# One small expert in plain fp32 and a shorter largest expert, in the second layer of an attention and two-MoE kernel

## The chip, the cores and the metric

One core of a Trainium2 chip runs the whole kernel. The metric is the device time of one execution in microseconds. Three runs of the kernel before gave 630.59, 633.81 and 631.4 us, a median of 631.4. The profile comes from one further execution.

## The reference, cut to what matters

Attention over chunks of 32 tokens is followed by two mixture-of-experts layers on 1536 tokens of 512 numbers, with 8 experts of 512 x 1024 and 1024 x 512 weights each. The first layer gives each token to two experts. The second one, which the change touches, gives each token to one:

```python
def _moe2_ref(x, w_gate, w1, w2, capacity):
    logits = x @ w_gate
    expert_idx = np.argmax(logits, axis=1)
    ...
    gate_w = probs[np.arange(N), expert_idx]
    ...
    h = np.maximum(np.einsum('ecd,edf->ecf', disp, w1), 0.0)
    y = np.einsum('ecf,efd->ecd', h, w2)
    ...
            out[i] = gate_w[i] * y[expert_idx[i], pos[i]]
```

The capacity is 384 tokens an expert. With the reference's inputs the second layer's experts get 215, 120, 35, 306, 113, 213, 369 and 165 tokens.

## The kernel before, in words

**Experts as jobs.** Each expert is a `Job` with a fixed number of slots, gathered by token number from DRAM into tiles `xg` of 128 rows. In the second layer one expert (369 tokens here) is done first, in two jobs. The other seven are ranked by their counts on the chip, and rank `s` gets `CAPS2[1 + s]` slots. They run in the order `ORDER2 = [0, 5, 1, 6, 2, 3, 4]`: the largest first, and the smallest (rank 6) fourth. Tokens that fit no slot would be done in blocks of 128 by `rest2` at the end, in a loop whose count is read from the data.

**Two kinds of job.** A product of fp32 numbers is made of three products of split ones: each operand is split into a high part `hi` in fp32r and a rest `lo`, and `mm3` (L804) adds lo x hi, hi x lo and hi x hi. A job of kind "M" (over 128 slots) does its first product by column blocks of the hidden layer, 8 units that stream the tokens (`layer1`, L815), and its second by blocks of 128 tokens, two units each, that stream 512 weight columns (`rows2`, L860). A job of kind "T" (up to 128 slots) has four units: `hidden` (L841) twice, with the tokens as stationary operand, 512 weight columns moving and a transposition `turn` (L849) of the result in the middle of the next unit, and `rows2` twice. After a unit, ScalarE takes the result out of PSUM (`hh`, `hr`, `hl` by VectorE), and `psA` has two buffers.

**Weights.** An expert's weights are four pieces of 1 MB. Piece n is loaded in two halves (`half`, L710) into four buffers `raww`, and split in four chunks (`split`, L738): ScalarE writes `whi`, VectorE `wlo`. Split pieces lie in five slots, "AAABC"[n % 5]. Which chunk is split after which unit of which job is a plan of numbers (`due`, L1667 to L1690); each second chunk then starts the load of the half four further on (`raw_next`). All weight loads are issued on SP's queue, gathers and scatters on POOL's.

**Order of the last jobs on TensorE's clock (us):** the largest ranked expert (384 slots) from 481.26, a 128-slot expert from 515.26, a 256-slot expert from 528.11, the smallest (128 slots) from 551.38, a 256-slot expert from 564.74, another from 588.54, and a 128-slot one from 611.50 to the end.

Of the kernel before, what the change touches and what calls it, by code (L numbers as in the profile page):

```python
# [8 lines left out]
F32 = mybir.dt.float32  # L9
# [3 lines left out]
I32 = mybir.dt.int32  # L13
# [2 lines left out]
AX = mybir.AxisListType  # L16

CAPS1 = [128, 432, 412, 404, 396, 384, 384, 384, 312]
CAPS2 = [256, 384, 256, 256, 256, 128, 128, 128, 128]
ORDER2 = [0, 5, 1, 6, 2, 3, 4]  # L20
NEG = -1.0e30
WARM = 7
# [32 lines left out]
def attention_two_moe_kernel(  # L55
# [698 lines left out]
    def x_block(xg, blk, C, tag="B", later=False):  # L754
        n = min(128, C - 128 * blk)
        p = bank(tag)
        pv = p.rearrange("p (k n) -> p k n", k=KD)
        for c in range(KD):
            nc.tensor.transpose(pv[:, c, 0:128], xg[:, c * 128:(c + 1) * 128], ident)  # L759
        o = slice(128 * blk, 128 * blk + n)  # L760
        xh, xl = st["x"]
        nc.scalar.activation(xh[:, :, o], pv[:, :, 0:n], AF.Copy)  # L762
        low = lambda: nc.vector.tensor_tensor(xl[:, :, o], pv[:, :, 0:n], xh[:, :, o], op=OP.subtract)  # L763
        if not later:
            low()
        return low
# [74 lines left out]
    def hidden(w, c, n, between=None):  # L841

        ps = bank("A")
        xh, xl = st["x"]
        mm3(ps[:n], [((xh[:, k, 0:n], xl[:, k, 0:n]), (w[0][:, k], w[1][:, k])) for k in range(KD)],
            between=between, order=RO)
        nc.scalar.activation(st["hr"][:n, 512 * c:512 * c + 512], ps[:n], AF.Relu)

    def turn(c, n):  # L849
# [7 lines left out]
        nc.scalar.activation(hh[:, o, 0:n], pv[:, :, 0:n], AF.Copy)  # L857
        nc.vector.tensor_tensor(hl[:, o, 0:n], pv[:, :, 0:n], hh[:, o, 0:n], op=OP.subtract)

    def rows2(n0, blk, half_, C, between=None):  # L860

        n = min(128, C - 128 * blk)
        s_ = slice(128 * blk, 128 * blk + n)
        if half_ == 0:
            st["l2"] = bank("C")
        hh, hl = st["h"]
        w = P[n0 + 2 + half_]
        mm3(st["l2"][:n], [((hh[:, 4 * half_ + f, s_], hl[:, 4 * half_ + f, s_]), (w[0][:, f], w[1][:, f]))
                           for f in range(4)], half_ == 0, half_ == 1, between, RO)
# [21 lines left out]
    def scatter(yr, n, ids_ap, first, prev):  # L891
        off = bass.IndirectOffsetOnAxis(ap=ids_ap[:n], axis=0)
        nc.gpsimd.memset(spacer, 0.0)
        if first:
            wr = nc.gpsimd.indirect_dma_start(out=x2_d, out_offset=off, in_=yr[:n], in_offset=None,  # L895
                                              compute_op=OP.add)
        else:
# [44 lines left out]
    class Job:  # L942


        def __init__(self, kind, n0, C, first, ids=None, gate=None, cols=None):
            self.kind, self.n0, self.C, self.first = kind, n0, C, first
            self.nb = -(-C // 128)
            self.ids, self.gate, self.cols, self.oids = ids, gate, cols, None
            self.W = W1 if first else W2
            self.late = None  # L950
            self.turns = {"W": [8, 10, 12, 14], "M": [8, 9, 10, 11], "T": TT}[kind]
            self.xg = None
            self.later = []
            self.pops = 4 if kind == "T" else 1
            self.quiet = 0 if kind == "T" else 1
            self.pool = ()
            self.weigh = 1 if kind == "T" else 5
            self.prev = []
            self.g = []
# [7 lines left out]
                self.xg.append(x)  # L967

        def x_block(self, blk, tag="B", gate=True):
            x_block(self.xg[blk], blk, self.C, tag)  # L970
            if gate:
                self.weight(blk)

# [26 lines left out]
        def units(self):  # L1000
            n0, C = self.n0, self.C
            if self.kind == "T":
                def between(c):
                    turn(c, C)
                    self.mid(c + 0.5)
                return [lambda: hidden(P[n0], 0, C), lambda: hidden(P[n0 + 1], 1, C, lambda: between(0)),
                        lambda: self.rows(0, 0, lambda: between(1)), lambda: self.rows(0, 1)]
# [288 lines left out]
    blkb = iota([128, NB1], [[128, NB1]], 0, 0, "blkb")  # L1296
    trash = iota([128, NB1 // 4, 4], [[0, NB1 // 4], [128, 4]], 0, 1, "trash")
    trash = trash.rearrange("p a b -> p (a b)")
    spacer = consts.tile([1, 1], F32, name="spacer")
    blank(1, nc.gpsimd)  # L1300
    v_blank(1)
# [58 lines left out]
    st["h"] = (wp["B"].tile([128, FB, CM], F32R, name="hh"), wp["B"].tile([128, FB, CM], F32R, name="hl"))  # L1360
    st["hr"] = wp["B"].tile([128, FF], F32, name="hr")
    st["yt"] = wp["B"].tile([128, KD, 128], F32, name="yt")
    st["y"] = (wp["B"].tile([128, KD, CM], F32R, name="yh"), wp["B"].tile([128, KD, CM], F32R, name="yl"))

    n2 = 4 * E
# [2 lines left out]
    kind2 = lambda c: "T" if c <= 128 else "M"  # L1368
    U0 = Job("M", n2, caps2[0], False, gate=lambda xg, g: gate2(xg, None, g))
    UL = Job("T", n2, caps2[E], False, gate=U0.gate)  # L1370
    R = [Job(kind2(caps2[1 + s]), n2 + 4 + 4 * i, caps2[1 + s], False, gate=U0.gate) for i, s in enumerate(ORDER2)]
    jobs = [V0, V8, *S, U0, UL, *R]
    at = {job: j for j, job in enumerate(jobs)}
# [218 lines left out]
    def chain2():  # L1592
        lt = late()
        w = ""
        while w != "counted":
            w = next(lt)
            if w != "counted":
                yield w
        yield "d"
        yield from turns(h_rank2(), lt)  # L1600
        kept = rt.tile([128, U0.nb], I32, name="kept")
        nc.vector.tensor_tensor(kept, tab2[:, E, 0:U0.nb], trash[:, 0:U0.nb], op=OP.add)
        ids, raw_ids = yield from slot_ids(tab2[:, 0:E], st["sel2"], E, NB2, "2")
        for job, s in zip(R, ORDER2):
            job.ids = [ids[:, s, b:b + 1] for b in range(job.nb)]
        for h in range(2 * n2 + 10, 2 * n2 + 12):
            raw(h, True)
        oids_u = out_ids(kept, tab2[:, E, 0:U0.nb], [128, U0.nb], rt, "u")
        U0.oids = [oids_u[:, b:b + 1] for b in range(U0.nb)]
        for f in U0.later:  # L1610
            f()
        yield "d"
        oids = out_ids(ids, raw_ids, [128, E, NB2], rt, "2")
        for job, s in [(UL, E - 1)] + list(zip(R, ORDER2)):
            job.oids = [oids[:, s, b:b + 1] for b in range(job.nb)]
        R[0].fetch()
# [51 lines left out]
        plan.setdefault((at[job], u), []).extend(what)  # L1668

    split_q += [(3, c) for c in range(4)]  # L1670
    for job in jobs[1:-1]:
        n = job.n0
        four = lambda m: [(m, c) for c in range(4)]
        if job is V8:
            todo_, us = four(4) + four(5) + four(6), [7, 7, 8, 8, 9, 9, 10, 11, 12, 13, 14, 15]
        elif job is U0:
            todo_, us = four(n + 3), [0, 1, 2, 3]
        elif job is UL:
            todo_, us = four(n + 4) + four(n + 5) + four(n + 6), UU
        elif job.kind == "T":  # L1680
            todo_, us = four(n + 4) + four(n + 5) + four(n + 6), US
        elif job.kind == "M":
            todo_ = sum((four(n + 3 + i) for i in range(4)), [])
# [5 lines left out]
        if job in R and jobs[at[job] + 1].kind == "T":  # L1689
            due(job, 6 + 2 * job.nb, *four(n + 7))  # L1690
    def raw_next(h):
        if h >= 8 and not 2 * n2 + 4 <= h < 2 * n2 + 8:
            raw(h + 4)

    run_jobs(jobs, hooks, lambda j, u: plan.get((j, u), []), raw_next)
    rest2(w1b, w2b, ov[2], en2, NB2)
# [36 lines left out]
```

## Time and profile before

| | |
|---|---|
| median of three runs | 631.4 us (630.59 to 633.81) |
| the profiled execution | 632.0 us |
| its span | 630.2 us |
| TensorE (PE) busy | 595.4 us, 94% of the span |
| VectorE (DVE) busy | 384.1 us, 61% |
| ScalarE (ACT) busy | 311.2 us, 49% |
| GpSimd (POOL) busy | 165.0 us, 26% |
| mean granted TensorE clock | 0.972 of 2.4 GHz |
| moved by DMA | 112.13 MB, mean 178 GB/s |

The span runs from the first to the last instruction of the profiled execution; its own time is 1.8 us longer. Busy times are sums over instructions with overlaps counted once. The page shows PE busy in nearly every slice of the second half, so what matters there is how long each stage of TensorE's work takes and where it waits.

### The profile page before, as it was taken

To read this page: it belongs to the slowest core of one execution; us is meant where nothing else is said; L and a number is where in the kernel's file an instruction comes from. 1 tells how busy PE (TensorE), PEld (TensorE's weight loads), DVE (VectorE), ACT (ScalarE), POOL (GpSimd) and SP (SyncE) were. 2 spreads that over 40 slices of the span, in tenths; PEclk is the share of its full clock that TensorE was granted. 3 is DMA by queue.
4 is the path that set the end of the run, shared out by engine and by line. 5 is a ranking of instruction groups with operands and counts; after the bars stand their busy time and mean duration, and the time that the engine had idled before them with its cause. 6 is when DMAs were issued, how large, how long until landed. Compare 5 with 4: busy or idle time off the path is not lost. (4 is left out here: it accounts for less than half of the span.)

```text
span 630.2 us, 12317 instructions
## 1 busy us (share of the span) xinstructions
PE 595.4 (94%) x4523; PEld 540.9 (86%) x4529; DVE 384.1 (61%) x1015; ACT 311.2 (49%) x653; POOL 165.0 (26%) x237
## 2 busy tenths in 40 slices
PE   7699869699999999999999999999999999999996
PEld 4688657499999999999999898988979988889984
DVE  8577754677645555555555447273557648687672
ACT  5265543225544544545445435344427557686563
POOL 8894000211411312313212130302351121111201
PEclk9799886899999999999999999999999999999999
DMA  9986670339775664856536565455366486776751
GB/s 252 269 142 197 214 234 20 88 99 345 222 221 168 174 185 149 221 152 135 170 103 151 166 142 165 107 121 151 38 235 215 152 264 220 251 273 234 247 182 41
DMA packets 77068, 112.13 MB, mean 178 GB/s; under 512 B 28353, under 2 KB 28353, under 8 KB 77000
## 3 DMA queue, kind: packets, MB, share of 16 engines
q1 hardware_dynamic: 68088, 88.99, 44.7%
q0 software_dynamic: 8912, 22.28, 15.7%
q8 instruction: 38, 0.62, 0.4%
q14 instruction: 30, 0.25, 0.1%
HBM read 88.90 MB, written 22.34 MB: 176 GB/s over the span
## 5 line engine op out<-in xcount | busy, mean ns | idle before, releaser
L746 DVE TENSOR_TENSOR wlo<-raww,whi 128x512 fp32r<-128x512 f32 x254 | 168.8, 688 | 44.1 <-ACT whi L745 42.7
L745 ACT ACTIVATE whi<-raww 128x512 fp32r<-128x512 f32 x256 | 152.2, 624 | 17.7 <-DMA raww<-in_moe_w_dram 14.9
L823 DVE SCALAR_TENSOR_TENSOR hl<-psA,hh 128x384 fp32r<-128x384 f32 (+6 forms) x104 | 54.0, 519 | 80.4 <-ACT hh L822 80.0
L822 ACT ACTIVATE hh<-psA 128x384 fp32r<-128x384 f32 (+6 forms) x104 | 47.7, 458 | 109.2 <-PE psA L811 109.2
L811 PE MATMUL psA<-xh,wlo 128*128 128x256 f32 (+6 forms) x416 | 85.8, 328 | 0.8 <-ACT xh L762 0.4
L811 PE MATMUL psA<-xh,whi 128*128 128x256 f32 (+6 forms) x416 | 83.7, 322 | 0.0
L811 PE MATMUL psA<-xl,whi 128*128 128x256 f32 (+6 forms) x416 | 83.6, 323 | 0.0
L895 POOL DMA_INDIRECT x_rows<-yr,ids x25 | 39.2, 1568 | 125.4 <-ACT whi L745 86.2
L811 PEld LDWEIGHTS psA<-xh,wlo 128*128 128x128 f32 x416 | 67.7, 190 | 2.4 <-ACT xh L762 0.8
L811 PEld LDWEIGHTS psA<-xl,whi 128*128 128x128 f32 x416 | 69.3, 189 | 0.6 <-DVEq L1098 0.2
L811 PEld LDWEIGHTS psA<-xh,whi 128*128 128x128 f32 x416 | 69.1, 189 | 0.4
L751 POOL DMA_INDIRECT xg<-x_rows,ids x37 | 37.1, 1002 | 100.7 <-DVE gs L931 41.1
L811 PE MATMUL psC<-wlo,hh 128*128 128x512 f32 x200 | 57.6, 407 | 0.0
L811 PE MATMUL psC<-whi,hh 128*128 128x512 f32 x200 | 55.6, 396 | 0.0
L811 PE MATMUL psC<-whi,hl 128*128 128x512 f32 x200 | 55.0, 395 | 0.0
L763 DVE TENSOR_TENSOR xl<-psB,xh 128x512 fp32r<-128x512 f32 (+4 forms) x37 | 23.9, 645 | 43.1 <-ACT xh L762 43.1
L811 PEld LDWEIGHTS psC<-whi,hh 128*128 128x128 f32 x200 | 37.4, 189 | 8.4
L811 PEld LDWEIGHTS psC<-whi,hl 128*128 128x128 f32 x200 | 37.5, 188 | 8.3
L762 ACT ACTIVATE xh<-psB 128x512 fp32r<-128x512 f32 (+4 forms) x37 | 20.7, 560 | 44.0 <-PE psB L759 41.8
L811 PEld LDWEIGHTS psC<-wlo,hh 128*128 128x128 f32 x200 | 35.4, 189 | 5.7
L898 POOL DMA_INDIRECT out_dram<-yr,oids x13 | 13.2, 1013 | 98.1 <-ACT yr L873 71.6
L811 PE MATMUL psA<-hh,wlo 128*128 128x312 f32 (+4 forms) x160 | 36.6, 350 | 0.0
(328 smaller groups left out, 913.3 us busy)
## 6 DMA issues: line engine op xcount, KB each, us to landing
raww<-in_moe_w_dram SPq DMA_DIRECT2D x128, 512.0 KB
x_rows<-zero SPq DMA_DIRECT2D x8, 520.0 KB
raw<-in_k_dram SPq DMA_DIRECT2D x6, 512.0 KB
raw<-in_q_dram SPq DMA_DIRECT2D x6, 512.0 KB
x_rows<-xs SPq DMA_DIRECT2D x12, 256.0 KB
out_dram<-zero SPq DMA_DIRECT2D x3, 1024.0 KB
v<-in_v_dram SPq DMA_DIRECT2D x10, 256.0 KB
x_rows<-zero SPq DMA_DIRECT2D x1, 1042.0 KB
```

What stands on the lines that cost most here:

```text
L745: nc.scalar.activation(hi[:, c], raw, AF.Copy)
L746: (eng or nc.vector).tensor_tensor(lo[:, c], raw, hi[:, c], op=OP.subtract)
L751: return nc.gpsimd.indirect_dma_start(out=xg, out_offset=None, in_=src, in_offset=bass.IndirectOffsetOnAxis(ap=ids_ap, axis=0))
L762: nc.scalar.activation(xh[:, :, o], pv[:, :, 0:n], AF.Copy)
L763: low = lambda: nc.vector.tensor_tensor(xl[:, :, o], pv[:, :, 0:n], xh[:, :, o], op=OP.subtract)
L811: nc.tensor.matmul(ps, w[a], x[b], start=first and i == 0, stop=last and i == n - 1)
L822: nc.scalar.activation(hh[:, f, 0:C], ps[:, 0:C], AF.Relu)
L823: nc.vector.scalar_tensor_tensor(hl[:, f, 0:C], ps[:, 0:C], 0.0, hh[:, f, 0:C], op0=OP.max, op1=OP.subtract)
L895: wr = nc.gpsimd.indirect_dma_start(out=x2_d, out_offset=off, in_=yr[:n], in_offset=None, compute_op=OP.add)
L898: wr = nc.gpsimd.indirect_dma_start(out=out, out_offset=off, in_=yr[:n, 0:DM], in_offset=None, bounds_check=N - 1, oob_is_err=False)
```

## The change

1. `CAPS2`: rank 0 gets 320 slots for 384, rank 6 gets 64 for 128.
2. The job with 64 slots is computed in plain fp32. `whole` loads each weight matrix as two tiles of 1 MB, unsplit, straight into the slots of pieces n and n+1; `halves` runs, for each of the row blocks, two matmuls with the same 64 tokens as stationary operand, one for the left 256 columns into partitions 0 to 63 of PSUM, one for the right 256 into 64 to 127. `hidden64`, `turn64` and `rows64` take the places of `hidden`, `turn` and `rows2`.
3. The tokens of that job are gathered twice (rows 0 to 63 and 64 to 127), and its output is scattered as half rows of 256 numbers with indices `2 * id + upper`.
4. The plan of splits is made to fit: pieces 50 and 51 are gone, the whole loads start during the 256-slot job ahead of the small one, and the 256-slot job behind it splits five pieces, not four.

```diff
-CAPS2 = [256, 384, 256, 256, 256, 128, 128, 128, 128]
+CAPS2 = [256, 320, 256, 256, 256, 128, 128, 64, 128]
+    def whole(n, two):
+        run_until(lambda: "C" in wp)
+        at_, ns = "AAABC"[n % 5], ("whi", "wlo")
+        P[n] = tuple(wp[at_].tile([128, 4, 512], F32, name=m, bufs=3 if at_ == "A" else 1) for m in ns)
...
+            nc.sync.dma_start(P[n][j], src)
+    def halves(ps, xs_, w, first, last, between):
+        for i, x in enumerate(xs_):
+            if between is not None and i == len(xs_) // 2:
+                between()
+            for d in range(2):
+                nc.tensor.matmul(ps[64 * d:64 * d + 64, 0:256], x, w[:, i, 256 * d:256 * d + 256],
+                                 start=first and i == 0, stop=last and i == len(xs_) - 1)
+            tick(0.4)
+    def hidden64(n0, c, between=None):
+        ps = bank("A")
+        halves(ps, [st["xf"][:, k] for k in range(KD)], P[n0][c], True, True, between)
+        nc.scalar.activation(st["hr"][:, 256 * c:256 * c + 256], ps[:, 0:256], AF.Relu)
+    def turn64(c):
+        p = bank("B")
+        for j in range(2):
+            nc.tensor.transpose(p[:, 128 * j:128 * j + 128], st["hr"][:, 256 * c + 128 * j:256 * c + 128 * j + 128],
+                                ident)
+        nc.scalar.activation(st["hf"][:, 4 * c:4 * c + 4].rearrange("p (d j) n -> p d j n", d=2),
+                             p[:, 0:256].rearrange("p (j d n) -> p d j n", j=2, d=2), AF.Copy)
+    def rows64(n0, c, between=None):
+        if c == 0:
+            st["l2"] = bank("C")
+        halves(st["l2"], [st["hf"][:, 4 * c + f] for f in range(4)], P[n0 + 1][c], c == 0, c == 1, between)
...
+        for t in (ids, raw_ids):
+            nc.vector.tensor_copy(t[64:128, HALF[0], 0:1], t[0:64, HALF[0], 0:1])
...
+        two = rt.tile([128, 1], I32, name="oids_h")
+        nc.vector.scalar_tensor_tensor(two, oids[:, HALF[0], 0:1], 2.0, upper, op0=OP.mult, op1=OP.add)
...
+    upper = iota([128, 1], [[0, 1]], 0, 1, "upper")
+    nc.gpsimd.tensor_scalar(upper, upper, 64.0, None, op0=OP.is_ge)
...
+    hook(R[HALF[1] - 1], 1, lambda: whole(nh, (HALF[0], 0)))
+    hook(R[HALF[1] - 1], 5, lambda: whole(nh + 1, (HALF[0], 1)))
...
+        elif job is hj:
+            todo_, us = four(n + 5), [1, 1.5, 2, 3]
...
+        elif jobs[at[job] + 1] is hj:
+            todo_, us = four(n + 3) + four(n + 8), [1, 2, 3, 4, 8, 9, 9, 10]
+        elif job.n0 == nh + 4:
+            todo_ = sum((four(n + 2 + i) for i in range(5)), [])
+            us = [0, 0, 1, 1, 2, 2, 3, 4, 5, 6, 7, 8, 8, 8, 9, 9, 10, 10, 11, 11]
...
-            raw(h + 4)
+            raw(h + 12 if 2 * nh - 4 <= h < 2 * nh else h + 4)
```

TensorE's order from the first matmul of the small expert to its second turning, in the kernel before (L811 is `mm3`, L855 `turn`, L759 the turning of the next expert's rows):

```order
L811 MATMUL psA<-wlo,xh 128x512 x4
L811 MATMUL psA<-whi,xh 128x512 x4
L811 MATMUL psA<-whi,xl 128x512 x4
L811 MATMUL psA<-wlo,xh 128x512 x4
L811 MATMUL psA<-whi,xh 128x512 x2
L855 MATMUL psB<-ident,hr 128x128 x4
L811 MATMUL psA<-whi,xh 128x512 x2
L811 MATMUL psA<-whi,xl 128x512 x4
L759 MATMUL psD<-ident,xg 128x128 x4
L811 MATMUL psC<-wlo,hh 128x512 x4
L811 MATMUL psC<-whi,hh 128x512 x2
L855 MATMUL psB<-ident,hr 128x128 x4
```

The small expert in the changed kernel, with the first matmuls of the next one at the end (L880 is `halves`, L894 `turn64`; whi and wlo hold the left and the right half of a weight matrix here):

```order
L880 MATMUL psA<-whi,xf 64x256 x8
L880 MATMUL psA<-wlo,xf 64x256 x4
L894 MATMUL psB<-ident,hr 128x128 x2
L880 MATMUL psA<-wlo,xf 64x256 x4
L759 MATMUL psD<-ident,xg 128x128 x4
L880 MATMUL psC<-whi,yt 64x256 x4
L894 MATMUL psB<-ident,hr 128x128 x2
L759 MATMUL psD<-ident,xg 128x128 x4
L880 MATMUL psC<-whi,yt 64x256 x4
L880 MATMUL psC<-wlo,yt 64x256 x8
L811 MATMUL psA<-xh,wlo 128x256 x4
```

48 matmuls of 512 columns and 16 transposes became 32 matmuls of 256 columns and 12 transposes; the transposes cut the new ones into four stretches.

ScalarE's order at the beginning of the 256-slot expert behind the small one, before (L745 is `split`, L822 the result of a `layer1` unit, L873 the small expert's rows):

```order
L873 ACTIVATE yr<-psC,gs 128x512
L745 ACTIVATE whi<-raww 128x512 x2
L822 ACTIVATE hh<-psA 128x256 x2
L745 ACTIVATE whi<-raww 128x512
L822 ACTIVATE hh<-psA 128x256
L745 ACTIVATE whi<-raww 128x512
L822 ACTIVATE hh<-psA 128x256
L745 ACTIVATE whi<-raww 128x512
L822 ACTIVATE hh<-psA 128x256
```

And in the changed kernel (L1069 is the small expert's rows):

```order
L1069 ACTIVATE yr<-psC,gs 128x256
L745 ACTIVATE whi<-raww 128x512
L822 ACTIVATE hh<-psA 128x256
L745 ACTIVATE whi<-raww 128x512 x2
L822 ACTIVATE hh<-psA 128x256
L745 ACTIVATE whi<-raww 128x512 x2
L822 ACTIVATE hh<-psA 128x256
L745 ACTIVATE whi<-raww 128x512 x2
L822 ACTIVATE hh<-psA 128x256
L745 ACTIVATE whi<-raww 128x512
L822 ACTIVATE hh<-psA 128x256
```

Each of the first three units is now followed by two conversions instead of one; VectorE's part `wlo` and its `hl` follow in the same order.

## Rows read from the trace of the kernel before

**Rows 1.** The page, busy us of an engine, its share and instructions.

```profile
PE 595.4 (94%) x4523; PEld 540.9 (86%) x4529; DVE 384.1 (61%) x1015; ACT 311.2 (49%) x653; POOL 165.0 (26%) x237
```

**Rows 2.** Windows over the second layer: stretch, length, busy us (instructions), clock, DMA.

```profile
core 0: us, PE busy (x) PEld busy (x) DVE busy (x) ACT busy (x) POOL busy (x), PEclk, DMA share, GB/s
481.00:498.00 17.00, 17.00 (x98) 16.93 (x97) 10.51 (x22) 8.70 (x20) 3.09 (x3) 1.00 0.65 218
...
528.00:551.00 23.00, 22.89 (x149) 20.64 (x148) 16.07 (x33) 14.27 (x32) 5.22 (x7) 1.00 0.78 261
```

**Rows 3.** Waits of PE from 400 to 632 us: total, times, longest.

```profile
PE psB L759 <- DMA xg<-x_rows,ids_ul: 0.9, 1, 0.9
...
PE psB L855 <- ACT hr L847: 0.3, 1, 0.3
```

**Rows 4.** Timeline of PE, largest expert: start, length, instructions, idle before.

```profile
481.26 0.86 PE L811 MATMUL psA<-xh,wlo 128*128 128x384 f32 x4
...
498.06 1.09 PE L811 MATMUL psC<-wlo,hh 128*128 128x512 f32 x4
```

**Rows 5.** Timeline of PE, first product of a 256-slot expert: first and next.

```profile
588.54 0.64 PE L811 MATMUL psA<-xh,wlo 128*128 128x256 f32 x4
...
599.90 1.14 PE L811 MATMUL psC<-wlo,hh 128*128 128x512 f32 x4
```

**Rows 6.** Timeline of PE, the smallest expert.

```profile
551.38 1.09 PE L811 MATMUL psA<-wlo,xh 128*128 128x512 f32 x4
...
556.01 0.66 PE L855 MATMUL psB<-ident,hr 128*128 128x128 f32 x4 [0.30 <-ACT hr L847]
...
557.90 0.60 PE L759 MATMUL psD<-ident,xg 128*128 128x128 f32 x4
558.26 1.18 PE L811 MATMUL psC<-wlo,hh 128*128 128x512 f32 x4
...
563.82 1.09 PE L811 MATMUL psC<-whi,hl 128*128 128x512 f32 x4
564.74 0.64 PE L811 MATMUL psA<-xh,wlo 128*128 128x256 f32 x4
```

**Rows 7.** Timeline of PE in the attention: scores (L242), transposes, attend (L283).

```profile
34.16 1.15 PE L242 MATMUL psA<-kt,qz 128*64 128x64 f32 x32
35.24 0.66 PE L209 MATMUL psB<-ident,raw 128*128 128x128 f32 x4
...
36.17 0.60 PE L269 MATMUL psB<-ident,sm 128*128 128x128 f32 x4
36.70 1.11 PE L283 MATMUL psC<-v,ex 64*32 64x65 f32 x64
```

**Rows 8.** Line 242, the scores: count, ns (least/median/most), first and last start.

```profile
L242 PEld LDWEIGHTS psA<-kt,qz x384: 132/138/227, 14.1 to 74.4; 128*64 128x64 f32 x192
L242 PE MATMUL psA<-kt,qz x384: 221/222/370, 14.1 to 74.4; 128*64 128x64 f32 x192
```

**Rows 9.** The page, costliest groups: busy us, mean ns, idle before.

```profile
L746 DVE TENSOR_TENSOR wlo<-raww,whi 128x512 fp32r<-128x512 f32 x254 | 168.8, 688 | 44.1 <-ACT whi L745 42.7
L745 ACT ACTIVATE whi<-raww 128x512 fp32r<-128x512 f32 x256 | 152.2, 624 | 17.7 <-DMA raww<-in_moe_w_dram 14.9
```

**Rows 10.** Timeline of ACT shortly before the smallest expert.

```profile
550.54 1.15 ACT L745 ACTIVATE whi<-raww 128x512 fp32r<-128x512 f32 x2 [2.23 <-DMA raww<-in_moe_w_dram]
```

**Rows 11.** Timeline of all engines at a 256-slot expert's beginning.

```profile
530.75 0.42 DVE L823 SCALAR_TENSOR_TENSOR hl<-psA,hh 128x256 fp32r<-128x256 f32 x1
531.16 0.38 ACT L822 ACTIVATE hh<-psA 128x256 fp32r<-128x256 f32 x1 [0.85 <-PE psA L811]
531.23 0.54 PEld L811 LDWEIGHTS psA<-xh,wlo 128*128 128x128 f32 x4 [0.32 <-DVE hl L823]
```

**Rows 12.** Timelines: POOL's first gather and its use on PE; POOL at the start.

```profile
464.59 0.98 POOL L751 DMA_INDIRECT xg<-x_rows,ids  x1 [0.31 <-issue]
...
473.95 0.60 PE L759 MATMUL psD<-ident,xg 128*128 128x128 f32 x4
...
15.63 0.32 POOL L1306 COPY wg<-wg 128x4 f32<-128x4 f32 x2 [1.68 <-DMA wg<-in_moe_w_gate_dram]
```

More of the change, by code (lines that the diff above doesn't have):

```diff
@@ L858, in turn @@
         nc.vector.tensor_tensor(hl[:, o, 0:n], pv[:, :, 0:n], hh[:, o, 0:n], op=OP.subtract)
+    def whole(n, two):
+        run_until(lambda: "C" in wp)
+        at_, ns = "AAABC"[n % 5], ("whi", "wlo")
+        P[n] = tuple(wp[at_].tile([128, 4, 512], F32, name=m, bufs=3 if at_ == "A" else 1) for m in ns)
+        r = st["regs2"](two[0])
+        sl = ds(r, 1) if not isinstance(r, int) else slice(r, r + 1)
+        for j in range(2):
+            if two[1] == 0:
+                src = w1b[sl].rearrange("e (k p) f -> p (e k) f", p=128)[:, :, 512 * j:512 * j + 512]
+            else:
+                src = w2b[sl].rearrange("e (k p) f -> p (e k) f", p=128)[:, 4 * j:4 * j + 4, :]
+            nc.sync.dma_start(P[n][j], src)
[13 more added lines that the diff above has]
+        p = bank("B")
+        for j in range(2):
+            nc.tensor.transpose(p[:, 128 * j:128 * j + 128], st["hr"][:, 256 * c + 128 * j:256 * c + 128 * j + 128],
[6 more added lines that the diff above has]
+        halves(st["l2"], [st["hf"][:, 4 * c + f] for f in range(4)], P[n0 + 1][c], c == 0, c == 1, between)
     def rows2(n0, blk, half_, C, between=None):
@@ L896, in scatter @@
                                               compute_op=OP.add)
+        elif first is None:
+            wr = nc.gpsimd.indirect_dma_start(out=out.rearrange("n (h d) -> (n h) d", h=2), out_offset=off,
+                                              in_=yr[:, 0:256], in_offset=None,
+                                              bounds_check=2 * N - 1, oob_is_err=False)
         else:
@@ L949, in __init__ @@
             self.W = W1 if first else W2
+            self.whole = C == 64
             self.late = None
@@ L969, in x_block @@
         def x_block(self, blk, tag="B", gate=True):
-            x_block(self.xg[blk], blk, self.C, tag)
+            if self.whole:
+                p = bank(tag)
+                for c in range(KD):
+                    nc.tensor.transpose(p[:, 128 * c:128 * c + 128], self.xg[0][:, c * 128:(c + 1) * 128], ident)
+                nc.scalar.activation(st["xf"], p.rearrange("p (k n) -> p k n", k=KD)[:, :, 0:64], AF.Copy)
+            else:
+                x_block(self.xg[blk], blk, self.C, tag)
             if gate:
@@ L1003, in between, with end @@
                 def between(c):
-                    turn(c, C)
+                    if self.whole:
+                        turn64(c)
+                    else:
+                        turn(c, C)
                     self.mid(c + 0.5)
+                if self.whole:
+                    def end():
+                        rows64(n0, 1)
+                        yr = wp["B"].tile([128, W2], F32, name="yr", bufs=3)
+                        nc.scalar.activation(yr[:, 0:256], st["l2"][:, 0:256], AF.Copy, scale=self.g[0])
+                        scatter(yr, 128, self.oids[0], None, self.prev)
+                    return [lambda: hidden64(n0, 0), lambda: hidden64(n0, 1, lambda: between(0)),
+                            lambda: rows64(n0, 0, lambda: between(1)), end]
                 return [lambda: hidden(P[n0], 0, C), lambda: hidden(P[n0 + 1], 1, C, lambda: between(0)),
@@ L1362, in attention_two_moe_kernel @@
     st["yt"] = wp["B"].tile([128, KD, 128], F32, name="yt")
+    st["hf"] = st["yt"].rearrange("p k (j n) -> p (k j) n", n=64)
+    st["xf"] = wp["B"].tile([128, KD, 64], F32, name="xf")
     st["y"] = (wp["B"].tile([128, KD, CM], F32R, name="yh"), wp["B"].tile([128, KD, CM], F32R, name="yl"))
@@ L1370, in attention_two_moe_kernel @@
     UL = Job("T", n2, caps2[E], False, gate=U0.gate)
+    HALF = [(s, i) for i, s in enumerate(ORDER2) if caps2[1 + s] == 64][0]
+    nh = n2 + 4 + 4 * HALF[1]
     R = [Job(kind2(caps2[1 + s]), n2 + 4 + 4 * i, caps2[1 + s], False, gate=U0.gate) for i, s in enumerate(ORDER2)]
@@ L1615, in chain2 @@
             job.oids = [oids[:, s, b:b + 1] for b in range(job.nb)]
+        two = rt.tile([128, 1], I32, name="oids_h")
+        nc.vector.scalar_tensor_tensor(two, oids[:, HALF[0], 0:1], 2.0, upper, op0=OP.mult, op1=OP.add)
+        R[HALF[1]].oids = [two]
         R[0].fetch()
@@ L1688, in attention_two_moe_kernel @@
             due(job, u, x)
-        if job in R and jobs[at[job] + 1].kind == "T":
+        if job in R and jobs[at[job] + 1].kind == "T" and jobs[at[job] + 1] is not hj:
             due(job, 6 + 2 * job.nb, *four(n + 7))
```

1 line of the change is left out of this document (added).

## The prediction, made before the changed kernel ran

> **What bounds the kernel now.** I read the page's busy table first. It gives TensorE (PE) 94% of the span and no other engine more than 61% [rows 1]; a busy share alone proves nothing, so the stage comes next. The windows over the second layer show PE busy for 17.00 of 17 us and 22.89 of 23 us, at a granted clock of 1.00 [rows 2]. That is the upper of the two levels, 2.4 GHz. The waits of PE decide it: between 400 and 632 us the longest two are 0.9 and 0.3 us [rows 3]. So each microsecond that TensorE no longer needs after 481 us should come off the end, unless a new wait takes its place. ScalarE and VectorE matter only where they let TensorE wait, the DMA queue only where it lets ScalarE wait.
>
> **The largest expert, 384 to 320 slots.** Its first product is 96 matmuls (8 column blocks, 4 row blocks, 3 terms). They run from 481.26 to 498.06 us, so 0.175 us each at 384 columns [rows 4]. The same 96 at 256 columns run from 588.54 to 599.90 us, 0.1183 each [rows 5]. 320 lies halfway: 0.1467, so 96 x 0.0283 = **2.7 us less**. The second product is done in row blocks that stream 512 weight columns whatever their height. The third block falls from 128 to 64 rows but keeps its 24 matmuls: I take 0, between 0.3 less (shorter weight loads) and 0.3 more (two changes of tile shape, priced below).
>
> **The small expert.** Now it lasts 551.38 to 564.74 us, 13.36 us [rows 6]. Of that 48 matmuls at 0.23 (four in 0.92 at 563.82) are 11.0, 16 transposes at 0.09 (four in 0.36 at 557.90) are 1.4, the wait for hr is 0.30, and 0.6 is small change.
>
> Afterwards there are 32 plain-fp32 matmuls of 256 columns, each with 64 stationary columns, alternating between the two halves of the array. The attention scores of this very kernel have that shape with 64 moving columns. The trace counts 384 records for the program's 192 such matmuls [rows 8], so two records each, and 64 records for the new expert. 32 records begin at 34.16, the last ends at 35.31 and lasts 0.22: 0.93 us over 31 steps, 0.030 us a record [rows 7]. A transpose is an fp32 record too, over the full width: four take 0.60 with one lasting 0.27, so 0.109 us for 128 columns, 0.055 for 64. The scores go at about half of that, so their two halves do run side by side. Four times the columns is 0.109 + 0.003 = 0.112 if 3 ns of the 30 are fixed, and 0.120 if all scales: 64 records are 7.2 to 7.7 us. Between transposes the new order has four stretches, and at the ends of each one half is empty for a record: 4 x 0.11 = 0.5. I take 7.9. From below, at most 14 ns can be fixed (the 64 records at 36.70 go at 0.9/63); then a record is 0.014 + 4 x 0.016 = 0.078 and the total 5.0. From above, no overlap at all: 64 x 0.218 = 14.0.
>
> Each change between full width and half width costs something: the transposes at 35.24 begin 0.15 us after the last score began, where 0.03 is the pace; the ones at 36.17 are followed after 0.20 where 0.11 is the pace [rows 7]. So about 0.12 each, and the new order changes eight times: 1.0. Transposes fall from 16 to 12, 1.1. With 0.3 of small change it is 7.9 + 1.0 + 1.1 + 0.3 = 10.3, **3.1 us less**. The old wait for hr came behind four split conversions queued on ScalarE; here none is due in front of it.
>
> **The weights.** Sixteen splits go away, 0.62 us of ScalarE and 0.69 us of VectorE each [rows 9], about 10 and 11 us of engines that don't set the end: nothing by itself. The four loads of 1 MB wait on SP for slots that TensorE frees: the first pair until the expert two places ahead has ended, the second until the first four units of the expert just ahead have. Behind them on SP stand raw loads that are due later anyway. That stage moves 6 MB instead of 5 in about 23 us, 260 GB/s where the same window had 261 [rows 2]. Each pair has some 20 us from there to its use (528 to 551, and 534 to 555 on the old clock). I cost them at nothing; if they came late, the first matmul of the small expert would wait, as ScalarE did for 2.23 us at 550.54 [rows 10].
>
> **The expert after it** pays. It converts 20 chunks instead of 16, and two in each of its first three units, where one stood before. A unit is 12 x 0.1183 = 1.42 us on TensorE. VectorE needs 0.42 for hl and 2 x 0.64 for the two, 1.70: it falls behind by 0.28 us a unit. The two buffers of psA allow about 0.4 of that (an estimate: 1.42 less 0.38 for hh, 0.42 for hl and some 0.2 to hand over). Before, the same boundary already lost 0.28 (PE began at 531.23 behind hl) [rows 11]. Three units make 0.84 of lag; I take **0.5 us more**, between 0 and 2.2, the late raw of [rows 10].
>
> **Routing and start.** Two copies and one index operation of about 0.2 us each join VectorE's chain before the first gather, which is issued at 464.59; its rows are turned only at 473.95, behind work in order on TensorE, so 0.6 us hide [rows 12]. Two small operations on POOL at the start fall before its 1.68 us of idle time at 15.63 [rows 12]. Nothing.
>
> **Sum.** -2.7 - 3.1 + 0.5 = -5.3 us. The profiled execution took 632.0, 1.8 above its span; it becomes 626.7. The median of the three runs is 631.4, 0.6 lower, so I forecast **626.1 us**. A measurement of this kernel can tell about 0.5%, 3.2 us, from no change.
>
> **Rivals.**
> 1. *Late weights.* The expert after the small one gets its second matrices through four raw buffers that refill while it converts two chunks a unit. If one lands late, ScalarE stops in front of the next hh and TensorE behind it. For it: the 2.23 us at 550.54 happened while conversions were bunched. Against it: TensorE lost only 0.30 by that. Price 2.4 us: 628.5. Chance 0.10.
> 2. *The halves take turns.* Then 14.0 replaces 7.9, +6.1: 632.2, no change. Against it stands the pace of the scores; for it, that 64 columns are short and no long fp32 stream is in the trace. Chance 0.07. The Trainium skill ("FP8 and Floating Point Precision", TensorE Precision Notes) says that true fp32 takes four passes through the array. By that alone 32 x 4 x 256 columns at 2.4 GHz are an estimated 13.7 us against 48 x 512 columns, 10.2 us, for the split form, so it speaks against this change. The trace agrees on the passes (0.109 us for 128 columns in one record is two clocks a column), and only the side-by-side halves turn the sum round.
> 3. *Weight loads stand bare* (slower). All 128 rows are used by both halves. If a load couldn't run beside a matmul of the other half, a record would cost 0.218 plus 0.138 of load [rows 8]: 64 x 0.356 = 22.8, +14.9: 641.0. It turns into a loss once a record costs over 0.21 us on average. Against it: at 0.030 us a score record, loads of 0.138 must overlap. Chance 0.06. The Trainium skill ("TensorE: Matmul & The Clock Gate", Part 3) states that weight loads overlap matmuls in flight only when the row groups differ. By that rule this rival would hold, and the pace of the scores disagrees with it.
>
> That the change doesn't apply is out: the reference's routing of its inputs gives the largest ranked expert 306 tokens and the smallest 35, so neither cap overflows and the loop for leftovers stays empty.
>
> **The numbers.** Forecast 0.77, rivals 0.10, 0.07, 0.06. Faster by over 0.5% is the forecast alone: 0.77. Within 0.5% are rivals 1 and 2: 0.17. Slower: 0.06. The low end takes part of the cheap record (2.5 less): 623.6. The high end takes rival 1 and the spread of the runs, a little over 1 us: 629.6. It leaves out rivals 2 and 3 and thin tails, under 0.2.
>
> **What would show it.** The first stage of the largest expert lasts 14.1 instead of 16.8 us; the small expert 10.3 instead of 13.4, its 64 records starting about 0.11 us apart with two under way at once; a wait of psA behind hl of some 0.5 us in the next expert; no wait of the small expert's first matmul for whi or wlo. A pace of 0.22, or PE waiting on DMA at that place, would make it wrong.

## The result, and the profile after

The changed kernel takes 624.99 us, the median of six runs (621.48 to 626.54), against 632.12 us for the kernel before (six runs, 630.59 to 633.81). The ratio is 0.9899, with a 95% interval of 0.9866 to 0.9932: it is faster by about 1%. The profiled execution took 624.37 us, 1.9 above its span of 622.5. Medians and ratios in what follows leave out executions more than 1.5% above the fastest of the same kernel, which are one of 632.49 us of the kernel with both small edits (the one that its second profile shows) and one of 632.13 us of the changed kernel.

The page's busy table and its two groups of splits, against [rows 1] and [rows 9]:

```profile
PE 589.3 (95%) x4535; PEld 530.8 (85%) x4541; DVE 371.3 (60%) x999; ACT 301.5 (48%) x637; POOL 165.3 (27%) x239
...
L746 DVE TENSOR_TENSOR wlo<-raww,whi 128x512 fp32r<-128x512 f32 x238 | 158.6, 688 | 49.8 <-ACT whi L745 48.6
L745 ACT ACTIVATE whi<-raww 128x512 fp32r<-128x512 f32 x240 | 143.3, 624 | 14.8 <-DMA raww<-in_moe_w_dram 11.7
```

VectorE has 12.8 us less to do, ScalarE 9.7 and TensorE 6.1. The idle time ahead of VectorE's part of the splits grew from 44.1 to 49.8 us, that ahead of ScalarE's part fell from 17.7 to 14.8. Of the three, only TensorE's work can set the end. The windows over the largest expert's first product and the 256-slot expert ahead of the small one, against [rows 2]:

```profile
480.00:494.00 14.00, 14.00 (x97) 14.00 (x96) 9.33 (x20) 7.75 (x18) 3.08 (x3) 1.00 0.72 251
524.00:547.00 23.00, 22.89 (x149) 20.63 (x148) 11.90 (x27) 10.71 (x25) 5.20 (x7) 1.00 0.98 357
```

TensorE is as full as before, at the upper clock level. The last two columns show where the unsplit weights went: in the second window the DMA engines are busy 0.98 of the time at 357 GB/s, where 0.78 and 261 stood (8.2 MB in 23 us, where it was 6.0). The waits of PE from 400 to 625 us, against [rows 3]:

```profile
PE psB L759 <- DMA xg<-x_rows,ids_ul: 1.0, 1, 1.0
...
PE psB L855 <- ACT hr L847: 0.4, 1, 0.4
```

This list of waits has no new entry. The 0.4 us for hr now lies in the last 128-slot expert, at 608.43; the one of the small expert [rows 6] is gone. The timeline of PE (start, length, instructions) from the largest expert on, against [rows 4] and [rows 6]:

```profile
479.91 0.75 PE L811 MATMUL psA<-xh,wlo 128*128 128x320 f32 x4
...
494.07 1.09 PE L811 MATMUL psC<-wlo,hh 128*128 128x512 f32 x4
...
508.41 1.09 PE L811 MATMUL psC<-wlo,hh 128*64 128x512 f32 x4
...
547.43 1.95 PE L880 MATMUL psA<-whi,xf 128*64 128x256 f32 x16
549.21 1.03 PE L880 MATMUL psA<-wlo,xf 128*64 128x256 f32 x8
550.17 0.44 PE L894 MATMUL psB<-ident,hr 128*128 128x128 f32 x2
550.54 1.08 PE L880 MATMUL psA<-wlo,xf 128*64 128x256 f32 x8
551.55 0.66 PE L759 MATMUL psD<-ident,xg 128*128 128x128 f32 x4
552.14 1.08 PE L880 MATMUL psC<-whi,yt 128*64 128x256 f32 x8
...
554.88 1.90 PE L880 MATMUL psC<-wlo,yt 128*64 128x256 f32 x16
556.70 0.75 PE L811 MATMUL psA<-xh,wlo 128*128 128x256 f32 x4
```

The largest expert's first product is 494.07 - 479.91 = 14.16 us, and the small expert 556.70 - 547.43 = 9.27. Of the 64-row blocks the rows say that four matmuls take 1.09, as with 128 rows. Read in this way stage by stage, the span of 630.2 us became 622.5:

| stage on TensorE, us | before | after | difference | predicted |
|---|---|---|---|---|
| up to the largest expert | 481.26 | 479.91 | -1.35 | 0 |
| its first product | 16.80 | 14.16 | -2.64 | -2.7 |
| its second product | 17.20 | 17.12 | -0.08 | 0 |
| the two experts behind it | 36.12 | 36.24 | +0.12 | 0 |
| the small expert | 13.36 | 9.27 | -4.09 | -3.1 |
| the 256-slot expert behind it | 23.80 | 23.76 | -0.04 | +0.5 |
| from there to the end | 41.66 | 42.04 | +0.38 | 0 |

The first line isn't put down to the change: in nine other traces of this study, whose first layer is the same work, the largest expert begins anywhere from 478.29 to 484.44. From its first matmul on the program became shorter by 148.94 - 142.59 = 6.35 us, where 5.3 were forecast.

The last line has a cause as well. The next 256-slot expert's first product lasts 11.75 us (580.46 to 592.21), where [rows 5] have 11.36. The 0.39 more lies in its first units:

```profile
582.83 0.64 PE L811 MATMUL psA<-xh,whi 128*128 128x256 f32 x4
583.58 0.74 PE L811 MATMUL psA<-xh,wlo 128*128 128x256 f32 x4
```

The four matmuls from 582.83 are followed after 0.75 us, where 0.47 is the pace. The weight loads of the next ones wait 0.32 us for hl, which VectorE begins at 583.11, behind two conversions begun at 581.90. The changed plan puts two splits after the last unit of the expert ahead (11, 11); the old plan had none there. All traces with the new small expert have 11.74 to 11.76 us here, those with the old one 11.36.

### The profile page after: what moved, and what is told of

Same layout as the page of the kernel before. It is cut to its first block, busy times and chain, and to the rows that moved or that the text cites. A ratio compares the mean times of both kernels' runs of the same rounds, so it can differ in the third digit from the quotient of the medians.

```text
span 622.5 us, 12283 instructions
## 1 busy us (share of the span) xinstructions
PE 589.3 (95%) x4535; PEld 530.8 (85%) x4541; DVE 371.3 (60%) x999; ACT 301.5 (48%) x637; POOL 165.3 (27%) x239
## 5 line engine op out<-in xcount | busy, mean ns | idle before, releaser
L746 DVE TENSOR_TENSOR wlo<-raww,whi 128x512 fp32r<-128x512 f32 x238 | 158.6, 688 | 49.8 <-ACT whi L745 48.6
L745 ACT ACTIVATE whi<-raww 128x512 fp32r<-128x512 f32 x240 | 143.3, 624 | 14.8 <-DMA raww<-in_moe_w_dram 11.7
L822 ACT ACTIVATE hh<-psA 128x256 fp32r<-128x256 f32 (+7 forms) x104 | 47.4, 455 | 105.7 <-PE psA L811 105.3
L823 DVE SCALAR_TENSOR_TENSOR hl<-psA,hh 128x256 fp32r<-128x256 f32 (+7 forms) x104 | 53.4, 513 | 74.9 <-ACT hh L822 74.5
L811 PE MATMUL psA<-xh,wlo 128*128 128x256 f32 (+7 forms) x416 | 85.3, 327 | 0.8 <-ACT xh L762 0.4
L811 PE MATMUL psA<-xh,whi 128*128 128x256 f32 (+7 forms) x416 | 82.8, 320 | 0.0
L811 PE MATMUL psA<-xl,whi 128*128 128x256 f32 (+7 forms) x416 | 82.7, 321 | 0.0
L811 PEld LDWEIGHTS psA<-xh,wlo 128*128 128x128 f32 x416 | 67.0, 190 | 2.9 <-ACT xh L762 0.8
L811 PEld LDWEIGHTS psA<-xl,whi 128*128 128x128 f32 x416 | 68.6, 189 | 0.6 <-DVEq L1165 0.2
L811 PEld LDWEIGHTS psA<-xh,whi 128*128 128x128 f32 x416 | 68.5, 189 | 0.3
L811 PE MATMUL psC<-wlo,hh 128*128 128x512 f32 (+1 forms) x192 | 55.1, 406 | 0.0
L811 PE MATMUL psC<-whi,hh 128*128 128x512 f32 (+1 forms) x192 | 53.2, 395 | 0.0
L811 PE MATMUL psC<-whi,hl 128*128 128x512 f32 (+1 forms) x192 | 52.9, 395 | 0.0
L811 PEld LDWEIGHTS psC<-whi,hh 128*128 128x128 f32 (+1 forms) x192 | 35.4, 186 | 8.6
L811 PEld LDWEIGHTS psC<-whi,hl 128*128 128x128 f32 (+1 forms) x192 | 35.5, 186 | 8.4
L811 PEld LDWEIGHTS psC<-wlo,hh 128*128 128x128 f32 (+1 forms) x192 | 33.4, 186 | 5.8
L811 PE MATMUL psA<-hh,wlo 128*128 128x312 f32 (+4 forms) x160 | 36.7, 351 | 0.0
```

What stands on the lines that cost most here:

```text
L745: nc.scalar.activation(hi[:, c], raw, AF.Copy)
L746: (eng or nc.vector).tensor_tensor(lo[:, c], raw, hi[:, c], op=OP.subtract)
L811: nc.tensor.matmul(ps, w[a], x[b], start=first and i == 0, stop=last and i == n - 1)
L822: nc.scalar.activation(hh[:, f, 0:C], ps[:, 0:C], AF.Relu)
L823: nc.vector.scalar_tensor_tensor(hl[:, f, 0:C], ps[:, 0:C], 0.0, hh[:, f, 0:C], op0=OP.max, op1=OP.subtract)
```

## The experiments

**Each half of the change alone.** The kernel before with only the largest expert's slots changed, and the changed kernel with that line put back:

```diff
-CAPS2 = [256, 384, 256, 256, 256, 128, 128, 128, 128]
+CAPS2 = [256, 320, 256, 256, 256, 128, 128, 128, 128]
```

> The largest expert alone gets 320 slots; the small one stays as before with 128 slots in split form. Theory (TensorE sets the end, each stage counts by its own length): the first product of the largest expert lasts 14.2 us instead of 16.8, the small expert stays at 13.4, the total falls by 2.7 us (0.43%). Rival (the whole gain hangs on the small expert or on the conversions it saves): no gain.

Measured: 629.0 us (10 runs) against 631.4 for the kernel before, ratio 0.9955 (0.9924 to 0.9986). The first product lasts 14.16 us, 2.64 less. But the small expert, untouched here, lasts 14.26 us instead of 13.36. The timeline of PE in this kernel shows why (in brackets the idle time before, and its releaser):

```profile
557.41 0.66 PE L855 MATMUL psB<-ident,hr 128*128 128x128 f32 x4 [1.20 <-ACT hr L847]
```

The wait for hr has grown from 0.30 to 1.20. ScalarE stands before it with bunched split conversions that wait for raw weights; its longest wait of that kind in this stretch grew from 2.2 to 2.8 us, as the waits of ACT (total, times, longest) from 480 to 600 us show:

```profile
ACT whi L745 <- DMA raww<-in_moe_w_dram: 4.0, 3, 2.8
```

So in this trace late weights do cost TensorE time, but in the *old* form of the small expert, and more than before, now that TensorE needs less time to get there.

```diff
-CAPS2 = [256, 320, 256, 256, 256, 128, 128, 64, 128]
+CAPS2 = [256, 384, 256, 256, 256, 128, 128, 64, 128]
```

> The small expert alone is changed; the largest keeps 384 slots. Theory: the small expert's stage lasts 9.3 us as in the changed kernel, the total falls by 4.1 us (0.65%), and with the kernel with 320 slots alone this adds up to the whole gain. Rival (the two parts help each other, or one of them only gives room to the other): the two parts don't add up to the whole, by more than 1 us.

Measured: 628.15 us (10 runs), ratio 0.9959 (0.9925 to 0.9992); first product 16.80, small expert 9.27. The two stages that the change is about, 14.16 and 9.27, last as long with the other part as without it. The two times, 2.4 and 3.2 us below the kernel before, make 5.6 together, where the whole change has 7.1; with about 2 us of uncertainty on either side of each, they can't tell whether the parts add up. The traces can: from the largest expert's first matmul to the end it is 147.50 us with the largest expert's cap alone and 144.93 with the small expert alone, 1.44 and 4.01 below the 148.94 of before. That is 5.45 together where the whole has 6.35. The missing 0.90 is what the old small expert loses in the first of the two kernels, by the longer wait for hr.

**Fewer slots without the new form.** The kernel before with 64 slots for the smallest rank, still split:

```diff
-CAPS2 = [256, 384, 256, 256, 256, 128, 128, 128, 128]
+CAPS2 = [256, 384, 256, 256, 256, 128, 128, 64, 128]
```

> The kernel before with the small expert's cap at 64, still in split form with 128-slot code paths (64 stationary columns, 512 moving ones, full-width order). Theory (a matmul costs its moving columns, not its stationary ones): 48 matmuls at 0.23 us remain, the stage stays at 13.0 to 13.4 us and the total within 0.5 us of the kernel before. Rival (the smaller cap itself is the gain): the stage falls to 10 us or less.

Measured: 633.23 us (10 runs), ratio 1.0034 (0.9998 to 1.0071), 1.9 us above the kernel before where at most 0.5 was expected. The trace puts none of that into the second layer's last experts: from the largest expert's first matmul to the end it has 148.85 us, before 148.94. Two rows of the timeline of PE say why nothing is won:

```profile
553.65 1.09 PE L811 MATMUL psA<-wlo,xh 128*64 128x512 f32 x4
...
566.70 0.52 PE L811 MATMUL psA<-xh,wlo 128*128 128x256 f32 x3
```

With 64 stationary columns four matmuls still take 1.09 us, since 512 weight columns stream past them. The stage lasts 13.05 us, the 0.31 less lies around the transposes, where the wait for hr is gone. The gain of the small expert comes from the form of the product, not from the smaller cap.

**The halves one after the other.** The loops of `halves` are turned round, so that the program gives all matmuls of the left half ahead of those of the right:

```diff
-        for i, x in enumerate(xs_):
-            if between is not None and i == len(xs_) // 2:
+        for d in range(2):
+            if between is not None and d == 1:
                 between()
-            for d in range(2):
+            for i, x in enumerate(xs_):
                 nc.tensor.matmul(
...
-            tick(0.4)
+                tick(0.2)
```

> The changed kernel, but the small expert's matmuls are ordered so that all four row blocks of the left half come before those of the right half; the number of matmuls is the same. Theory (the gain comes from two halves of the array under way at once): consecutive records are on the same half and go one after the other at about 0.213 us; 64 records with four places where the half changes inside a stretch are 60 x 0.213 = 12.8 us instead of 6.7, without the half-empty ends (0.4): the stage lasts about 15 us, and the total is 5 to 6 us longer than the changed kernel's. Rival A (256 columns of 64 stationary ones simply cost 0.105 us a record, whichever half): no difference. Rival B (weight loads stand bare as soon as two records share a half): 0.213 + 0.137 a record, the stage lasts over 22 us.

Measured: 629.53 us (10 runs), ratio 0.9968 (0.9940 to 0.9997), and a small expert of 12.93 us, 3.66 more with the same 64 records. It fell short of full serialisation, and the timeline of PE shows where:

```profile
549.53 2.21 PE L880 MATMUL psA<-whi,xf 128*64 128x256 f32 x13
551.37 0.43 PE L880 MATMUL psA<-wlo,xf 128*64 128x256 f32 x1
551.58 0.38 PE L880 MATMUL psA<-whi,xf 128*64 128x256 f32 x1
551.64 0.38 PE L880 MATMUL psA<-wlo,xf 128*64 128x256 f32 x1
...
553.61 1.94 PE L880 MATMUL psA<-wlo,xf 128*64 128x256 f32 x8
...
562.46 0.75 PE L811 MATMUL psA<-xh,wlo 128*128 128x256 f32 x4
```

Left and right are here the two halves of the array, whose results go to partitions 0 to 63 and 64 to 127; each of the tiles whi and wlo has columns for both, and whi's work stands first in the program. A matmul from wlo begins at 551.37, before whi's last three, although all of whi's stand ahead of it in the program. Records don't name their half; which one each belongs to is read from the program's order and the even steps of the starts. Read so, the single records show the same inside the first row: the left half's eight start 0, 0.27, 0.48, 0.70, 0.91, 1.13, 1.35 and 1.56 us after the first, and the right half's first starts at 0.92, with three of the left still to come. Each half goes at 0.216 us a record, with or without the other at work. Where only one half has work (x8, 1.94 us at 553.61) the time is nearly double that of the changed kernel (x8, 1.08 at 550.54).

So the halves of the array do work side by side, and that is worth at least 3.66 us here, since some of it is left in this kernel too. In this order the change to the small expert is worth only 13.36 - 12.93 = 0.43 us. With nothing side by side it would be slower than the old form: 64 x 0.216 = 13.8 in place of 6.9 makes the stage about 16.2 us, an estimate from these rows.

**Loads at the last moment.** In the changed kernel the four unsplit loads are issued at the end of the expert ahead, not near its beginning:

```diff
-    hook(R[HALF[1] - 1], 1, lambda: whole(nh, (HALF[0], 0)))
-    hook(R[HALF[1] - 1], 5, lambda: whole(nh + 1, (HALF[0], 1)))
+    hook(R[HALF[1] - 1], 11, lambda: whole(nh, (HALF[0], 0)))
+    hook(R[HALF[1] - 1], 11, lambda: whole(nh + 1, (HALF[0], 1)))
```

> The changed kernel with the four 1 MB loads of the unsplit weights issued after the last unit of the expert ahead, in place of its second and sixth. Theory (the loads cost nothing because they have some 20 us of cover; they move at 350 to 400 GB/s): they are issued about 4 to 5 us before the small expert begins, 1 MB lands every 2.7 us, so TensorE waits for whi at the stage's first matmul (0 to 2 us) or later for the second matrix (1 to 4 us), 1 to 5 us in all. Rival (loads of this size never reach TensorE, since the queue is idle there): no wait and a stage of 9.3 us.

One execution: 634.49 us (628.51 for the kernel before, beside it). The loads go out from 547.64 us on, and the first is in use at 554.50. The timeline of PE, and windows over the wait and the work after it (length, busy us, the clock third from the end):

```profile
547.72 1.08 PE L811 MATMUL psC<-whi,hl 128*128 128x512 f32 x4
554.50 3.68 PE L880 MATMUL psA<-whi,xf 128*64 128x256 f32 x16 [5.71 <-DMA whi<-in_moe_w_dram]
557.94 1.90 PE L880 MATMUL psA<-wlo,xf 128*64 128x256 f32 x8
...
560.14 1.08 PE L880 MATMUL psA<-wlo,xf 128*64 128x256 f32 x8
```

```profile
550.00:554.40 4.40, 0.00 (x0) 0.00 (x0) 0.00 (x0) 0.00 (x0) 0.87 (x2) 0.82 0.99 330
554.40:558.00 3.60, 3.50 (x18) 2.15 (x20) 0.00 (x0) 0.00 (x0) 0.00 (x0) 0.50 1.05 405
...
562.00:566.00 4.00, 4.00 (x38) 2.56 (x34) 3.27 (x7) 2.98 (x6) 0.00 (x0) 1.00 0.04 13
```

The loads bring 5.71 us of wait, more than the 1 to 5 expected, and then a second bill that no expectation had: after that idle time the granted clock is 0.50, the lower level, and the first 24 records take 5.28 us instead of 2.74. The stage itself lasts 11.81 us, 2.54 more than 9.27, and all of that is in those 24 records. In the changed kernel the last load is issued at 534.90, 12.5 us ahead of its stage, and none of this occurs.

**The changes of width, and the splits behind.** Two small edits, alone and together. The first puts both turnings of the next expert's rows into one place, beside the second turning of the small expert's own result, so that the second product follows the first directly. This takes one of the three gaps away (`one_gap`). The second spreads the split conversions of the expert behind, one after each unit from the second on (`one_split_a_unit`):

```diff
     hj = R[HALF[1]]
+    hj.turns = [1.5, 1.5]
...
-            us = [0, 0, 1, 1, 2, 2, 3, 4, 5, 6, 7, 8, 8, 8, 9, 9, 10, 10, 11, 11]
+            us = [0, 1, 2, 3, 4, 5, 6, 7, 8, 8, 8, 8, 9, 9, 9, 10, 10, 10, 11, 11]
```

> The changed kernel with both turnings of the next expert's rows in one gap, beside the second turning of the small expert's own result, so that the 64-column matmuls are cut into three stretches, not four. Theory (each gap costs about 0.24 us beyond its transposes, 0.09 going into full width and 0.15 coming back, and about 0.05 for the first record of a stretch): the stage falls from 9.27 to about 9.0 us. Rival (the gaps are waits for ScalarE's results, which stay): 9.2 us or more, or longer, if hr or xl comes late.

> The changed kernel with the conversions of the expert behind the small one spread as one a unit in its first eight units (the rest bunched behind). Theory (two conversions a unit let VectorE fall behind and TensorE wait for hl, 0.4 us in all in the changed kernel): its first product falls from 11.79 us to 11.4 to 11.6 us (an opening wait behind the small expert's last conversions may stay), and the second product stays at 11.97. Rival (the bunched conversions behind are late for the next expert): the next expert's first product, 11.75 now, grows by over 0.3 us.

> Both of the two kernels' edits at once: one gap fewer in the small expert, and one conversion a unit in the next. Theory: both stages keep their gains, the small expert at about 9.0 us and the next one's first product at 11.4 to 11.6. Rival (the two share a cover on ScalarE): one of the two gains is gone.

One execution of each took 626.19, 628.2 and 625.26 us; as times these say nothing, given the spread of single executions. The stages do:

| us | changed | one gap | one split a unit | both |
|---|---|---|---|---|
| small expert | 9.27 | 8.97 | 9.27 | 8.97 |
| first product behind it | 11.79 | 11.79 | 11.48 | 11.46 |

The timeline of PE with both edits, in the middle of the small expert, shows the eight transposes in one piece and the two stretches around it:

```profile
553.18 1.03 PE L880 MATMUL psC<-whi,yt 128*64 128x256 f32 x8
554.15 0.44 PE L894 MATMUL psB<-ident,hr 128*128 128x128 f32 x2
554.42 1.04 PE L759 MATMUL psD<-ident,xg 128*128 128x128 f32 x8
555.39 1.08 PE L880 MATMUL psC<-whi,yt 128*64 128x256 f32 x8
```

A gap for a pair of changes of width thus costs 0.30 us, and bunched splits cost 0.31 in the product behind. The first product of the expert after that, 11.75 us in the changed kernel, stays at 11.76 with the splits spread and 11.75 with both edits: neither edit touches the delay found there above.

**Both edits and the changed kernel, timed together.**

> The kernel with one gap in the small expert (all first-product records, then all second-product records after the middle work) and one split a unit, once more and timed. By its stages: small expert 8.97 us against the changed kernel's 9.27, first product behind it 11.46 against 11.79, so about 0.6 us (0.1%) below the changed kernel beside it, which the times can't resolve; 1.0 to 1.2% below the kernel before. Rival: the 0.6 us is taken back in front of or behind these stages; then the small expert and the next first product are short again, but the stretch from the start of the small expert to the end of the program is as long as the changed kernel's.

> The changed kernel itself, on the same chip as the one above, for more runs of both: 1.0% below the kernel before (0.7 to 1.3%), small expert 9.27 us, largest expert's first product 14.16, first product behind the small expert 11.8. Rival: if these stages differ by more than 0.1 us from the first profile, the comparisons by stages have less weight than I give them.

Measured: 623.54 us for the one with both edits (5 runs), ratio 0.9891 (0.9859 to 0.9924); 624.9 for the changed kernel (11 runs), ratio 0.9923 (0.9894 to 0.9952). The stages repeat: 8.97 and 11.46 with the edits, 9.28 and 11.79 without. From the small expert's first matmul to the end of the span it is 73.69 and 74.34 us in the two traces with both edits, 75.07 and 74.88 in the two without, at a granted clock of 0.98 or 0.99 in all four. So the version with both edits is ahead of the changed kernel by its stages, but the two intervals overlap and the times don't show it.

## Why the prediction was right, and where it was off

**Direction and mechanism: right.** TensorE sets the end after 481 us, and both stages that were to become shorter did. The forecast of 626.1 us is 1.1 above the median of 624.99, and the second set of runs gave 624.9.

**The largest expert: right.** -2.7 was forecast, -2.64 came, from the pace at 384 and at 256 columns alone. The block of 64 rows was costed at nothing and is nothing: -0.08.

**The small expert: right in kind, 1.0 us too dear.** The 64 records with their half-empty ends were to cost 7.9 us. They cost 32 x 0.216 = 6.9, and 0.05 more at the first record of each of the four stretches, 7.1 in all. The starts show two records under way at once, 6 to 7 ns apart (0, 7, 267, 273, 482, 489, 698, 705 ns after the first). The step that failed is "at the ends of each one half is empty for a record: 4 x 0.11 = 0.5". No half is ever empty: the first records of both halves start together, though the program gives the left half's two records before the right half's first. The scores in the kernel before do the same, with starts at 34.160 and 34.166, so this could have been read beforehand. The pace of 0.108 a record lies a little below the 0.112 to 0.120 that was taken from the scores. By the prediction's own reckoning some 4 ns of the scores' 30 are then fixed (4 x 0.026 + 0.004 = 0.108), where it took 3 or none. Changes of width came to 0.8 (three gaps of 0.244 beyond their transposes, 0.09 at the end) where 1.0 was taken, transposes to 12 x 0.109 = 1.3 for 1.1, and the 0.3 of small change has no counterpart.

**The expert behind: the delay is real, but it replaced another, which moved on.** I forecast 0.5 us more and got 0.05 more in the first product (11.79 for 11.74). The delay is there: against 96 x 0.1183 = 11.36 the first product loses 0.43, and the one with one split a unit 0.12. What I left out is that the kernel before lost 0.38 at this very place, by another wait of the same kind. Its timeline of all engines:

```profile
563.67 3.81 DVE L746 TENSOR_TENSOR wlo<-raww,whi 128x512 fp32r<-128x512 f32 x6
...
567.39 0.42 DVE L823 SCALAR_TENSOR_TENSOR hl<-psA,hh 128x256 fp32r<-128x256 f32 x1
...
567.86 0.54 PEld L811 LDWEIGHTS psA<-xh,wlo 128*128 128x128 f32 x4 [0.32 <-DVE hl L823]
```

VectorE came out of six conversions in a row and was late with hl. The change took those away and put three smaller delays of about 0.1 us each in their place. I had read that loss at the boundary of another expert [rows 11] and compared the new delay with a product that has none [rows 5], not with the one that it replaces. Nor is the old delay gone: the plan now bunches two splits after the last unit of the expert behind, and the 0.39 us shows up in the first product of the next one, where the forecast had nothing. The two experts together lose 0.05 + 0.39 = 0.44 in their first products, close to the 0.5 forecast, but partly in another place, so that agreement is luck.

**Weights and routing: right, with the traffic too low.** The forecast of 6 MB and 260 GB/s for the stage of the loads was too small, 8.2 MB and 357 GB/s came, but the loads land in time. The late-loads kernel shows that the cover is needed: without it 5.71 + 2.54 = 8.25 us go in the one execution profiled, more than the 6.35 that the change brings.

**The rivals.** *Late weights* (628.5) didn't occur in the changed kernel: the waits of PE name no raw weights, and ScalarE's waits for them from 480 to 600 us, 3.1 us before, are gone. A wait of that kind exists, as the kernel with only the largest expert's cap changed shows for the old small expert. *The halves take turns* (632.2) is refuted by the pairs of starts and the stage of 9.27 us, and the kernel that makes them take turns in part pays 3.66 us. *Weight loads stand bare* (641.0) is refuted by the line of the new matmuls, which lists both kinds of record (count, ns least/median/most):

```profile
L880 PEld LDWEIGHTS psA<-whi,xf x16: 132/137/137, 547.4 to 548.8; 128*64 128x64 f32 x16
L880 PE MATMUL psA<-whi,xf x16: 379/379/430, 547.4 to 549.0; 128*64 128x256 f32 x16
```

Two loads of 137 ns go with each pair of records that starts every 216 ns. If they stood bare, no such pace could be. The Trainium skill ("TensorE: Matmul & The Clock Gate", Part 3) says in its list of what overlaps that this happens only where the row groups differ; both halves here use all 128 rows, and the measurement decides against that sentence. The same part also names loads into a background weight buffer as an overlap; whether that is what happens here no run shows.

**The first 480 us** gave 1.35 us in the profiled pair, inside the spread of where the largest expert begins, and count as luck. The runs of the same kernel spread over several us, so the agreement of forecast and median to 1.1 us says less than the stages do; there the forecast fell short of the gain by 1.05 us.

## What to carry to other kernels

A product with few rows that streams wide weights is paid by the streamed columns, so fewer slots alone saved only 0.31 us here; splitting the columns over the two halves of the array, with their matmuls alternating in the program, is what halves the bill of the plain fp32 product (0.108 us a record for 0.216), and plain fp32 also saves the conversions of split weights. When a change adds a delay, compare it with the delay at the same place in the kernel before, not with an undisturbed stage elsewhere, and look whether the old delay has only moved to the next stage. Keep the unsplit loads well ahead: the wait of 5.71 us here was paid twice, once as idle time and once as the lower clock behind it. The wait of 1.20 us for hr was paid once: the clock in the window from 556 to 560 us around it was 1.00.

## What the runs showed of the hardware that I had not expected

- A record of one half of the array can start ahead of records that stand before it in the program, if those belong to the other half: up to three in the kernel with the halves in turn, and by one record in the changed kernel, where starts lie 6 to 7 ns apart. The Trainium skill ("TensorE: Matmul & The Clock Gate", Part 3) says that matmuls start strictly in program order; the recorded starts here differ.
- After 5.71 us of idle time TensorE was granted 0.50 of its clock, and 24 records took 2.54 us longer than at the upper level.
- Executions differ ahead of the second layer's largest expert, not in it: it begins between 478.29 and 484.44 us in eleven traces, while its first product at 320 slots lasts 14.16 us in each of the eight of them that have it. The granted clock from 60 to 140 us is one thing that differs. In the changed kernel's second profile, whose largest expert begins at 478.29, it is 0.89; in the kernel with the halves in turn, where it begins at 482.01, it is 0.83:

```profile
60.00:140.00 80.00, 63.97 (x767) 55.19 (x768) 54.75 (x219) 30.15 (x76) 10.79 (x16) 0.89 0.47 145
```

```profile
60.00:140.00 80.00, 66.16 (x758) 56.23 (x757) 52.86 (x210) 28.98 (x73) 9.06 (x15) 0.83 0.45 141
```

  It isn't all: 0.83 also stands in the first profile of the changed kernel, where the largest expert begins at 479.91. Why executions differ stays open.
